# Running the later steps of eight attention items sooner, ahead of a woven MLP

## The chip, the cores and the metric

The kernel runs on one core of one Trainium2 chip. The metric is the device time of one execution in microseconds (us). PE is the matmul engine, DVE the vector engine, ACT the scalar engine, POOL GpSimd, SP the sync engine that issues most of the loads.

## What is computed

Causal attention with a decay bias, then a dense MLP with leaky ReLU, then a mixture of four experts that all see every token. Heads are joined into 1152 tokens of width 512 between attention and MLP.

```python
def _attn_ref(q, k, v, s):                      # q, k, v: (2, 8, 576, 64), s: (2, 8, 576)
    scores = scale * np.matmul(q, k.transpose(0, 1, 3, 2))
    cum = np.cumsum(np.maximum(s, 0.0), axis=-1)
    bias = -(cum[:, :, :, None] - cum[:, :, None, :])
    scores = np.where(causal, -1e9, scores + np.minimum(bias, 0.0))
    attn = np.exp(scores - np.max(scores, axis=-1, keepdims=True))
    attn = attn / (np.sum(attn, axis=-1, keepdims=True) + 1e-09)
    return np.matmul(attn, v)

def _moe_ref(x, w_in, w_out):                   # 512 -> 2048 -> 512
    h = x @ w_in
    return np.maximum(0.01 * h, h) @ w_out

def _moe2_ref(x, domain_probs, w1, w2):         # 4 experts, 512 -> 1024 -> 512
    p = domain_probs / (domain_probs.sum(-1, keepdims=True) + 1e-09)
    for e in range(4):
        out += p[:, e:e + 1] * (np.maximum(x @ w1[e], 0.0) @ w2[e])
```

## The kernel before

**Parts.** The tokens of each batch are cut into a first part (positions 0 to 255, two tiles of 128) and a second part (256 to 575, three tiles). A *unit* is one pair of heads of one batch in one part. Units 0 to 7 are the first part, units 8 to 15 the second. A unit is cut into *items*, one row tile of one head, or the short last tile of both heads together: four items in a unit of the first part (items 0 to 31), five in one of the second (items 32 to 71). Item 27 ends unit 6, item 31 ends unit 7 and with it the first part.

**Steps of an item** (class `Unit`). `scores` (line 691) multiplies on PE into a bank `ps_sc` (two of these) and lets DVE add the mask and take the row minimum of the negated scores. `exps` (line 718) is one ACT instruction. `transposes` (line 722) turns the tile on PE into a bank `ps_pt` (two of these, shared with `finish`), and ACT copies it out. `values` (line 732) multiplies with the values on PE into the one bank `ps_o`; at the last item of a unit DVE then divides by the row sums (`st`, `xo`). `finish` (line 749), which does something at the last item of a unit only, transposes the unit's output on PE (`ps_x`, a bank of `ps_pt`) and ACT writes it as the MLP's input `x`. `second_term` (line 770), for the first part and its last items only, lets DVE compute the rounding rest of that input, and counts the unit as done. None of these last four steps issues a DMA.

**Order.** All of this part is written into the engines in one order given by hand (`InOrder`, line 33): each engine works through its instructions strictly as they are written. `attention` (line 783) is a generator that counts i up from 0. At each i it writes `scores` of item i, `second_term` of item i - 8, `exps` of item i - 1, yields; `transposes` of item i - 3, yields; `values` of item i - 5, `finish` of item i - 7, yields. The list is `STEPS` (line 781); i runs to 79. Loads of keys and values follow i alone.

**First loop** (line 841). It draws the three yields of each i. Into the second one it puts one of nine early steps of the MLP (`OPENED`), which need only heads that are done; the tenth step needs the last pair of heads. From i = 31 it also puts one small matmul on zeros into the first and the second yield (`onto_held`, line 572: 128 columns, added onto a bank in use, where it changes nothing). After the third yield it advances the weight supply by one step from i = 31 on. It ends at the third yield of the i at which all eight units of the first part are done: `done == 2 * NP`.

**Weight supply.** `supply` (line 139) turns the 16 pieces of the first MLP's weights from 64-bit floats into 32-bit: ACT makes a first version, DVE works over it in four steps (`raw`), ACT's queue stores the piece to DRAM (`w_f`) and fetches the raw 64-bit bytes of a later piece. If the MLP is to use it soon, the piece is split at once into two terms (`w`). If not, `late_splits` (line 118) loads it back later by SP's queue and splits it. Piece 15 goes this second way.

**Second loop** (line 866). It draws the rest of attention, and per i weaves in about 2.12 steps of the MLP on the first part's tokens (`main`, 128 steps in all, three matmuls of 512 columns each), one to three supply steps and two of `late_splits`. It is called the weave below.

**Third loop** (line 885). It draws what is left of `main` with a count m from 0. At even m it advances `late_splits`; at every fourth m the ten steps of `tokens` (`paired_steps`, line 364), which prepare the second part's tokens for the next MLP on ACT and DVE (`sums` on DVE, `t` on both); at odd m from 5 the steps of `first_sevens` (line 213), which load two pieces by SP (pieces 16 and 17), add and subtract blocks of them on POOL (`sums`) and split them on ACT and POOL (`w`). What is left of either is written after the loop.

In `main`, the last parts are a down-projection (steps 88 to 103, results added to `y` by DVE), two hidden tiles (steps 104 to 111, evicted as `ht` by ACT and DVE), and the last down-projection (steps 112 to 127), which needs both hidden tiles and piece 15. Piece 15 may be split only once step 104 has been reached.

**Behind it** lies the MLP on the second part's tokens (matmuls `ps_u<-t,w`) and then the experts, ordered by a scheduler from its own estimates rather than by hand. The second of the seven products with which it begins needs the last step of `tokens`.

Of the kernel before, what the change touches and what calls it, by code (L numbers as in the profile page):

```python
# [19 lines left out]
def attention_moe_moe2(ctx: ExitStack, tc: tile.TileContext, q, k, v, s, w_in, w_out, probs, w1, w2, out):  # L20
# [36 lines left out]
    NP = H // 2  # L57
# [564 lines left out]
    def load_keys(n, queue=None):  # L622

        b, hp, i0, i1 = of_unit(n)
        q0, q1 = tiles[i0][0], tiles[i1 - 1][2]
        heads = slice(2 * hp, 2 * hp + 2)
        k_of = k[b, heads, :, :q1].rearrange("h d s -> d h s")
        q_of = q[b, heads, :, q0:q1].rearrange("h d s -> d h s")
        if i0 == 0:
            nc.sync.dma_start(k_e[n % 3][:D], k_of)  # L630
            (queue or nc.sync).dma_start(q_e[n % 3][:D], q_of)
        else:
            qr = ap.tile([P, 2, QC], F32, tag="qr", name="qr")
            for part in (slice(0, D), slice(D, P)):
                nc.sync.dma_start(qr[part, 0], q_of[:, 0])
                nc.sync.dma_start(qr[part, 1, LAST:], q_of[:, 1, : QC - LAST])
                nc.sync.dma_start(qr[part, 1, :LAST], q_of[:, 1, QC - LAST :])
            kr = ap.tile([P, 2, S], F32, tag="kr", name="kr")[:D]
            nc.sync.dma_start(kr, k_of)
            k_raw[n] = qr, kr  # L640

    def load_values(n, queue=None):
        b, hp, i0, i1 = of_unit(n)
        q1, rows, vs = tiles[i1 - 1][2], slice(hp * P, (hp + 1) * P), v_s[n % 4]
        full = min(q1 // P, QT - 1)
        (queue or nc.sync).dma_start(vs[:, :full, 1 : 2 * D + 1], v[b, : full * P, rows].rearrange("(t p) c -> p t c", p=P))
        if i1 == QT:
            nc.sync.dma_start(vs[P - S % P :, QT - 1, 1 : 2 * D + 1], v[b, full * P :, rows])
# [3 lines left out]
    def split_keys(n):  # L652

        b, hp = of_unit(n)[:2]
        qr, kr = k_raw.pop(n)
        qs = q_s[n % 2]
        ks, kd = (ap.tile([P, 2, S], F32R, tag=tag, name=tag) for tag in ("ks", "kd"))
        decay(n, kd)
        nc.gpsimd.dma_start(kd[:D], k[b, 2 * hp : 2 * hp + 2].rearrange("h d s -> d h s"))
        nc.scalar.copy(qs[:, 0, :, :QC], qr)  # L660
        yield
        nc.vector.tensor_tensor(qs[:D, 1, :, :QC], qr[:D], f32(qs[:D, 0, :, :QC]), ALU.subtract)
        for j in range(2):
            nc.scalar.copy(ks[:D, j], kr[:, j])
            yield
            nc.vector.tensor_tensor(ks[D:, j], kr[:, j], f32(ks[:D, j]), ALU.subtract)
        k_split[n] = ks, kd, qs
        yield

    def decay(n, kd):  # L670

        b, hp, i0, i1 = of_unit(n)
        q1, h = tiles[i1 - 1][2], b * H + 2 * hp
        if i0 == 0:
            nc.sync.dma_start(kd[D : D + 1], cum[h : h + 2, :q1])
        else:
            nc.sync.dma_start(f32(kd[D:DK, :, :q1]), cum_d[:, h : h + 2, :q1])
# [101 lines left out]


    STEPS = ((Unit.scores, 0), (Unit.second_term, 8), (Unit.exps, 1), (Unit.transposes, 3), (Unit.values, 5), (Unit.finish, 7))

    def attention():

        nonlocal ending
        items, starts, n = [], {}, 0
        i, split = 0, iter(())
        while n < units or i < len(items) + 8:
            if n < units and i == len(items):
                u = Unit(n)  # L790
                starts[n] = i
                items += [(u, *of) for of in u.items]
                if n + 2 < units and not 0 <= n + 2 - 2 * NP < 2:
                    load_keys(n + 2)
                    if n + 2 < 2 * NP:
                        decay(n + 2, k_e[(n + 2) % 3])
                if n in (2 * NP - 4, 2 * NP - 2):
                    load_keys(n + 4 if n == 2 * NP - 4 else n + 3)
                n += 1
            if n < units - 1 and i == starts[n - 1] + 2:  # L800
                load_values(n + 1)
            if i == starts[n - 1] and 2 * NP <= n < units:
                split = split_keys(n)
            for step, lag in STEPS:
                if 0 <= i - lag < len(items):
                    u, *of = items[i - lag]
                    step(u, *of)
                if lag == 1:
                    next(split, None)
                if lag in (1, 3, 7):  # L810

                    late = i - 5 + (lag == 7)
                    ending = lag != 3 and 0 <= late < len(items) and items[late][1:] == items[late][0].items[-1]
                    yield i
            i += 1
# [9 lines left out]
    with ExitStack() as phase:  # L825
# [5 lines left out]

        CONVERTING = (*range(5, 16), *range(17, 31, 2))
        side, units_of_w, late, opened = attention(), supply(), late_splits(), 0
        nothing = ps_mm.tile([P, 512], F32, tag="mm", name="nothing")
        with tc.tile_pool(name="early", bufs=1) as early:
# [5 lines left out]
            for at_ in range(3 * 64):  # L841
                i = next(side)
# [112 lines left out]
```

## Time and profile before

| what | us |
|---|---|
| median of three runs | 720.54 |
| the three runs | 717.39, 720.54, 970.85 |
| the profiled execution | 717.48 |
| its span in the profile | 715.70 |
| outside the span | 1.78 |
| end of the first loop (scores of item 40 begin on PE) | 69.55 |
| last matmul of attention begins | 195.96 |
| the next MLP begins on PE | 228.38 |

Times inside the profile count from the start of the span. A line of a timeline has start and duration, engine, operation with output and inputs, and how many instructions of a kind were merged (x3); square brackets hold the idle time of the engine before it and what ended that. All instructions bear the line of one helper (L43), so they are told apart by the names of their tiles. A matmul of plain 32-bit floats shows as two records, so an `onto_held` shows as x2.

### The profile page before, as it was taken

How to read it: one execution, taken by the hardware profiler on the slowest of the kernel's cores; microseconds unless marked ns; L12 is line 12 of the kernel's file. 1: busy time of each engine (PE TensorE's matmuls, PEld its weight loads, DVE VectorE, ACT ScalarE, POOL GpSimd, SP SyncE). 2: the span in 40 equal slices, each digit the busy share in tenths (PEclk: the TensorE clock that was granted, in tenths of full speed). 3: DMA queues.
4: the chain of work that ended last, by engine and by line, in shares of the span. 5: the costliest groups of instructions: out<-in, count | busy, mean ns of one | idle time of the engine just before them, and what ended most of it. 6: DMA issues, size and time to landing. Idle time of an engine off the chain costs nothing.

```text
span 715.7 us, 11167 instructions
## 1 busy us (share of the span) xinstructions
PE 696.9 (97%) x4256; PEld 633.2 (88%) x4256; DVE 433.7 (61%) x867; ACT 315.1 (44%) x640; POOL 253.9 (35%) x232
## 2 busy tenths in 40 slices
PE   8899999999988999999999999999999999999998
PEld 8778888888877999999988989889899898898986
DVE  7778788897767657735943634435435454364452
ACT  5757977875644574624422413323223142141210
POOL 6000000000039787964382522804526137142200
PEclk9999999999999999999999999999999999999999
DMA  9877688746442321320211211102011011010002
GB/s 232 207 195 208 194 211 245 220 143 235 177 177 61 118 82 66 119 60 30 60 60 31 59 31 59 60 1 89 31 57 54 8 60 60 1 59 1 1 36 97
DMA packets 43124, 69.61 MB, mean 97 GB/s; under 512 B 5616, under 2 KB 24832, under 8 KB 43072
## 3 DMA queue, kind: packets, MB, share of 16 engines
q1 hardware_dynamic: 32544, 40.83, 20.0%
q10 hardware_dynamic: 9376, 25.73, 10.6%
q0 software_dynamic: 1152, 2.36, 1.9%
q8 instruction: 33, 0.54, 0.3%
q14 instruction: 19, 0.16, 0.1%
HBM read 58.06 MB, written 10.82 MB: 96 GB/s over the span
## 4 chain that ended last, share of the span: by engine, by line
PE 82%; DVE 7%; DMA 4%; ACT 2%; POOL 2%; issue 1%; SPq 0%; ACTq 0%; POOLq 0%; DVEq 0%
PE ps_d L43 39%; PE ps_u L43 34%; PE ps_o L43 4%; PE ps_sc L43 3%; PE ps_pt L43 2%; DVE raw L43 2%; DMA qe<-in_q_dram 1%; DVE t L43 1%; ACT w L43 1%; DVE z L43 1%; DMA vs<-in_v_dram 1%; DMA raw<-w_f 1%; DMA ke<-in_k_dram 1%; DVE w L43 1%; POOL sums L43 1%
## 5 line engine op out<-in xcount | busy, mean ns | idle before, releaser
L43 PE MATMUL ps_u<-t,w 128*128 128x320 f32 (+1 forms) x1680 | 236.5, 299 | 1.1 <-DVE t L43 1.1
L43 PEld LDWEIGHTS ps_u<-t,w 128*128 128x128 f32 x1680 | 233.0, 189 | 4.8 <-DVE t L43 1.4
L43 PE MATMUL ps_d<-w,ht 128*128 128x512 f32 (+1 forms) x876 | 203.4, 388 | 0.0
L43 PEld LDWEIGHTS ps_d<-w,ht 128*128 128x128 f32 x876 | 161.0, 188 | 31.5
L43 POOL TENSOR_TENSOR w<-raw,w 128x512 fp32r<-128x512 f32 (+2 forms) x72 | 108.0, 1522 | 218.9 <-ACT w L43 218.9
L43 ACT ACTIVATE ht<-ps_u 128x320 fp32r<-128x320 f32 (+2 forms) x176 | 74.4, 433 | 153.7 <-DVE ps_u L43 129.0
L43 PE MATMUL ps_d<-ht,w 128*128 128x320 f32 (+1 forms) x576 | 111.0, 343 | 4.7 <-DVE ht L43 2.8
L43 DVE SCALAR_TENSOR_TENSOR oacc<-ps_d,pn,oacc 128x512 f32<-128x512 f32 (+1 forms) x64 | 47.5, 742 | 104.0 <-PE ps_d L43 104.0
L43 ACT CAST w<-raw 128x512 fp32r<-128x512 f32 (+2 forms) x94 | 64.5, 722 | 87.4 <-PE ps_d L43 67.7
L43 PEld LDWEIGHTS ps_d<-ht,w 128*128 128x128 f32 x576 | 92.3, 190 | 12.0 <-DVE ht L43 3.2
L43 DVE SCALAR_TENSOR_TENSOR ht<-ps_u,ht 128x320 fp32r<-128x320 f32 (+1 forms) x128 | 56.3, 452 | 23.3 <-ACT ht L43 22.0
L43 DVE TENSOR_TENSOR ps_u<-ps_u,tmp 128x320 f32<-128x320 f32 (+1 forms) x120 | 56.2, 471 | 23.3 <-PE ps_u L43 21.7
L43 POOL TENSOR_TENSOR sums<-raw 128x256 f32<-128x256 f32 x48 | 38.4, 818 | 66.1 <-PE ps_d L43 64.6
L43 DVE TENSOR_TENSOR tmp<-ps_u,tmp 128x320 f32<-128x320 f32 (+1 forms) x80 | 36.8, 463 | 40.4 <-PE ps_u L43 39.4
L43 POOL TENSOR_TENSOR w<-sums,w 128x1024 fp32r<-128x1024 f32 x24 | 58.2, 2424 | 5.3 <-ACT w L43 5.3
L43 PEld LDWEIGHTS ps_o<-vs,pv 128*128 128x128 f32 x400 | 53.5, 191 | 6.8 <-issue 2.3
L43 PE MATMUL ps_u<-x,w 128*128 128x512 f32 x192 | 56.3, 410 | 0.9 <-DVE x L43 0.9
L43 PE MATMUL ps_o<-vs,pv 128*128 128x65 f32 (+1 forms) x400 | 53.3, 267 | 2.1 <-DVE xo L43 1.2
L43 POOL DMA_DIRECT2D kd<-in_k_dram x8 | 4.8, 603 | 127.3 <-PE ps_sc L43 67.0
L43 ACT ACTIVATE z<-z,mn 128x256 f32<-128x256 f32 (+4 forms) x72 | 42.4, 588 | 12.0 <-DVE mn L43 7.2
L43 DVE CUSTOM_DVE_ANT_0 z<-ps_sc,mask 128x256 f32<-128x256 f32 (+4 forms) x72 | 36.0, 501 | 12.5 <-PE ps_sc L43 9.7
L43 ACT COPY pv<-ps_pt 128x512 f32<-128x512 f32 (+3 forms) x80 | 33.2, 424 | 21.2 <-PE ps_pt L43 20.7
(78 smaller groups left out, 647.0 us busy)
## 6 DMA issues: line engine op xcount, KB each, us to landing
raw<-in_moe_w_dram SPq DMA_DIRECT2D x32, 512.0 KB
raw<-w_f SPq DMA_DIRECT2D x22, 512.0 KB
r<-in_moe_w_in_dram ACTq DMA_DIRECT2D x8, 1024.0 KB
w_f<-raw ACTq DMA_DIRECT2D x16, 512.0 KB
r<-in_moe_w_out_dram ACTq DMA_DIRECT2D x8, 1024.0 KB
kd<-in_k_dram POOLq DMA_DIRECT2D x8, 288.0 KB, 6.0
kr<-in_k_dram SPq DMA_DIRECT2D x8, 288.0 KB
vs<-in_v_dram SPq DMA_DIRECT2D x8, 256.0 KB
```

What stands on the lines that cost most here:

```text
L43: ins = call(*args, **kw)
```

## The change

A function `sooner` says for items 24 to 31 (`left` from 7 down to 0) by how many i a step is drawn forward. For items 24 to 28: `values`, `finish` and `second_term` by one. For items 29 to 31: `transposes` by one, `values` by two, `finish` and `second_term` by three. `scores` and `exps` stay, and every other item stays. `attention` keeps for each step the next item that is due, and runs as many as are due.

```diff
     STEPS = ((Unit.scores, 0), (Unit.second_term, 8), (Unit.exps, 1), (Unit.transposes, 3), (Unit.values, 5), (Unit.finish, 7))
+    FIRST = 4 * 2 * NP
+
+    def sooner(n, step):
+
+        left = FIRST - 1 - n
+        if not 0 <= left < 8 or step in (Unit.scores, Unit.exps):
+            return 0
+        if left < 3:
+            return 1 if step is Unit.transposes else 2 if step is Unit.values else 3
+        return int(step is not Unit.transposes)
 
     def attention():
...
+        due = [0] * len(STEPS)
         while n < units or i < len(items) + 8:
...
-            for step, lag in STEPS:
-                if 0 <= i - lag < len(items):
-                    u, *of = items[i - lag]
+            for s, (step, lag) in enumerate(STEPS):
+                while due[s] < len(items) and i - due[s] >= lag - sooner(due[s], step):
+                    u, *of = items[due[s]]
                     step(u, *of)
+                    due[s] += 1
```

Unit 7 is therefore done at i = 36 and no longer at i = 39, and the first loop ends there.

## Rows read from the trace of the kernel before

**Rows 1.** Page: busy time, share of the span and instructions of each engine.

```profile
PE 696.9 (97%) x4256; PEld 633.2 (88%) x4256; DVE 433.7 (61%) x867; ACT 315.1 (44%) x640; POOL 253.9 (35%) x232
```

**Rows 2.** Windows by stage: length, busy PE, PEld, DVE, ACT, POOL; PE clock, DMA share, GB/s.

```profile
61.83:69.55 7.72, 7.72 (x65) 7.48 (x64) 6.96 (x17) 5.82 (x12) 0.02 (x1) 1.00 0.64 152
69.55:196.20 126.65, 124.59 (x783) 108.86 (x783) 105.76 (x197) 93.36 (x171) 2.90 (x5) 1.00 0.67 203
196.20:228.40 32.20, 27.53 (x115) 21.86 (x114) 23.99 (x32) 13.21 (x23) 20.16 (x17) 0.95 0.39 132
```

**Rows 3.** Timeline of PE, items 35 and 36.

```profile
57.60 0.66 PE L43 MATMUL ps_pt<-ident,z 128*128 128x128 f32 x4 [0.40 <-ACT pv L43]
59.18 0.30 PE L43 MATMUL ps_pt<-ident,z 128*128 128x128 f32 x1 [0.92 <-DVE x L43]
...
60.01 0.38 PE L43 MATMUL ps_u<-idle 128*128 128x128 f32 x2
60.23 0.33 PE L43 MATMUL ps_o<-vs,pv 128*128 128x65 f32 x2
```

**Rows 4.** Groups of DVE by form, 69.55 to 196.2 us: busy us, mean ns, idle before.

```profile
L43 DVE TENSOR_TENSOR ht<-ps_u,ht 128x512 fp32r<-128x512 f32 x14 | 9.6, 688 | 7.7 <-ACT ps_u L43 7.5
...
L43 DVE TENSOR_TENSOR w<-raw,w 128x1024 fp32r<-128x1024 f32 x7 | 8.6, 1224 | 4.5 <-ACT w L43 4.5
...
L43 DVE TENSOR_SCALAR raw<-raw 128x1024 f32<-128x1024 f32 x12 | 8.2, 686 | 0.0
```

**Rows 5.** Timeline of PE, end of the weave to the next MLP.

```profile
193.09 0.95 PE L43 MATMUL ps_u<-x,w 128*128 128x512 f32 x3
...
196.21 3.68 PE L43 MATMUL ps_d<-ht,w 128*128 128x512 f32 x15
201.76 5.71 PE L43 MATMUL ps_d<-ht,w 128*128 128x512 f32 x24 [1.88 <-DVE y L43]
207.31 5.60 PE L43 MATMUL ps_u<-x,w 128*128 128x512 f32 x24
212.75 2.71 PE L43 MATMUL ps_d<-ht,w 128*128 128x512 f32 x11
218.25 10.29 PE L43 MATMUL ps_d<-ht,w 128*128 128x512 f32 x37 [2.79 <-DVE ht L43]
```

**Rows 6.** Chain that ended last, 198 to 218 us: start, duration, what.

```profile
198.32 2.63 DMA w_f<-raw
...
201.45 5.91 DMA raw<-w_f
...
207.92 0.75 POOL sums L43
...
211.98 1.05 ACT w L43
...
214.23 3.37 DVE t L43
```

**Rows 7.** Timeline of ACT, 204 to 232 us.

```profile
207.38 1.66 ACT L43 CAST w<-raw 128x512 fp32r<-128x512 f32 x3 [7.24 <-DMA raw<-w_f]
...
221.16 1.05 ACT L43 CAST w<-sums 128x1024 fp32r<-128x1024 f32 x1 [5.14 <-POOL sums L43]
...
223.10 1.26 ACT L43 CAST t<-sums 128x1280 fp32r<-128x1280 f32 x1
```

**Rows 8.** Timeline of all engines, start of the next MLP.

```profile
228.38 11.89 PE L43 MATMUL ps_u<-t,w 128*128 128x320 f32 x80
...
229.19 1.69 DVE L43 TENSOR_TENSOR t<-sums,t 128x1280 fp32r<-128x1280 f32 x1
```

**Rows 9.** Windows of 4 us behind the second wait, columns as in rows 2.

```profile
216.00:220.00 4.00, 1.75 (x4) 1.41 (x5) 3.96 (x5) 0.01 (x1) 3.84 (x4) 0.80 0.28 57
220.00:224.00 4.00, 4.00 (x15) 3.19 (x14) 2.45 (x6) 2.84 (x4) 4.00 (x5) 0.78 0.02 3
```

**Rows 10.** Timeline of PE, 332 to 358 us, where the experts begin.

```profile
349.35 5.33 PE L43 MATMUL ps_u<-t,w 128*128 128x320 f32 x33 [1.15 <-DVE t L43]
```

## The prediction

> **What bounds the kernel now.** I read the page's busy shares first, then the windows by stage, then the timelines of PE and DVE where the first loop ends, and last the chain and the timelines where attention hands over to the next MLP. PE is busy 97% of the span [rows 1], so time is won only by taking work from PE or by closing a hole in it. The stages differ. In items 37 to 39, the last three of the first loop, PE has no hole in 7.72 us, yet six of its matmuls are fillers on zeros; DVE is busy for 6.96 of it [rows 2]. In the weave PE is busy 124.59 of 126.65 us. From its end to the next MLP, PE is busy 27.53 of 32.20 us, at a mean granted clock of 0.95 [rows 2]. There lie the two largest holes, 1.88 us for a bank that DVE frees and 2.79 us for a hidden tile that DVE finishes late [rows 5]. Behind the second, 37 matmuls take 10.13 us, 0.274 each, where 24 took 5.55, 0.231 each [rows 5]: the granted clock was 0.80 and 0.78 in the two stretches of 4 us there [rows 9], a mixture of its levels of 1.2 and 2.4 GHz.
>
> The chain says what set this. Piece 15's store leaves ACT's queue at 198.32 and takes 2.63; SP's load behind it takes 5.91; POOL's sums begin at 207.92; ACT splits them at 211.98, then casts `t`; DVE's `t` takes 3.37, and the hidden tile stands behind it [rows 6]. ACT itself stood 7.24 us for that load [rows 7].
>
> **The change part by part.**
>
> *The moved steps.* The same transposes, values and finishes run, none with a DMA, and they pass nothing but scores and fillers on PE. Item 31's `second_term` falls from i = 39 to 36, so the first loop ends three items sooner. Six fillers (two per i) go. From one pair's start to the next instruction is 60.23 - 60.01 = 0.22 us [rows 3]: 6 x 0.22 = 1.3 us off PE.
>
> *Items 28 to 36.* Two holes at item 35 should close: 0.40 us for a copy of ACT and 0.92 us for the bank that item 27's `second_term` frees [rows 3], now one item sooner. Gain at most 1.3. Against it, the division of unit 7 and item 31's rest now come to DVE before item 37 begins.
>
> *Items 37 to 39.* Seven steps of `main` join them: the weave runs 43 items instead of 40, at 2.12 steps. A step is 5.55 / 8 = 0.69 us [rows 5], so 4.8 us of PE work come here from the third loop. On DVE the stage gains three hidden tiles (3 x 0.69), one split (1.22) and two passes over a raw piece (2 x 0.69) [rows 4], 4.7 us, and loses unit 7's division and item 31's rest, together between nothing and as much as one split: 6.96 + 4.7 less 0 to 1.2 is 10.5 to 11.7 us beside 7.72 - 1.3 + 4.8 = 11.2 us of PE. DVE is all but full: its debt, with what items 28 to 36 leave it, costs PE between nothing and 1.2 us, one split. I take 0.6, the middle. With 0.6 of the possible 1.3 gained before, the front end nets 0, between -1.3 and +1.2.
>
> *DMA and weights.* Supply steps run sooner: three fewer in the first loop, seven more in the weave, so the supply is four steps ahead at a given i. Their stores and fetches on ACT's queue and the loads back on SP's move along, past attention's key loads. The DMA engines are 0.64 and 0.67 busy there [rows 2]: I cost this at nothing. Piece 4 is split two items ahead of its use where it was three; without that cover PE would wait for one split.
>
> *The third loop.* At the weave's end PE had 35 steps left from 197.6 us (196.21, and two steps of item 79 still of the weave). Without waits the next MLP would begin at 197.6 + 35 x 0.69 = 221.8; it began at 228.4 [rows 8]: 6.6 us lost in holes and clock. Now the weave ends at 197.6 - 1.3 + 4.8 = 201.1 with 28 steps left: 220.4 without waits. That is the ceiling, 8.0 us.
>
> What holds it back is the chain. Piece 15's store stood at item 78's second yield; four supply steps sooner, it stands at item 76's third. PE was there at 193.1 [rows 5], now 3.5 later, 196.6, 1.7 before 198.32. Loads land at 205.7 (207.4 less 1.7), POOL's first sums end at 210.3. The hidden tiles leave PE at m = 7 and m = 11, about 206.6 and 209.4, and now stand on ACT and DVE ahead of POOL's split and of the long `t`, since the counts m kept their places and `main` moved seven steps: both large holes should go. ACT splits piece 16 no sooner than before, having the second tile ahead of it; POOL, through its first sums 1.7 sooner, ends the second ones between 0 and 1.7 before 221.16 [rows 7]. I take 0.7, nearer to ACT's end: 220.4. From there ACT ends the last cast of `t` 3.2 later, as before (223.10 + 1.26 - 221.16 [rows 7]), at 223.6, and DVE the last `t` at 223.6 + 1.7 = 225.3 [rows 8]. Before, that came at 230.9, 2.5 us after the next MLP had begun, and delayed nothing. Now it is late next: PE arrives at 220.4, has 2.5 us of other products, and waits until 225.3, for 2.4 us. It gains 228.4 - 222.8 = 5.6 us. That new wait may bring the lower clock, which cost 37 x 0.043 = 1.6 after a like wait [rows 5, 9]; nothing at best. I take 0.6. Three steps of `tokens` are now left over after the loop instead of one: their time is in this sum.
>
> **Sum.** 5.6 - 0.6 + 0 = 5.0 us off the profiled execution's 717.5 (span 715.7 and 1.8 around it): 712.5 us. The median of the runs shown is 720.54, 3.1 above that execution, and one of the three stands far off, so I sum from the execution. Two per cent, 14 us, is what a measurement can tell here; nothing in this sum reaches it.
>
> The Trainium skill ("SBUF — State Buffer", Who interferes with whom) says that a DVE instruction with two SBUF inputs and a GpSimd instruction that reads SBUF take turns, whoever issued first holding the port to its end. The two long `t` of this trace, 3.37 and 1.69 us [rows 6, 8], are in keeping with that; it speaks against ending on a `t` beside POOL, and gives the second rival below.
>
> **Rivals.**
>
> *Only the fillers.* The third loop loses what it lost before, in other places: DVE's debt of 1.2 us carries through the weave, and the store is held there. For it: DVE is the engine nearest to full at the front. Against it: DVE is busy 105.76 of 126.65 us in the weave [rows 2], so a debt is paid back. Time: 717.5 - 1.3 = 716.2, up to 1.0 either way.
>
> *The last `t` meets POOL.* The long `t` of DVE took 3.37 us at 214.23, where POOL was at work nearly throughout, and 1.69 at 229.19 [rows 6, 8, 9]. After the change the last one falls at 223.6, when POOL still splits piece 17. If it takes 3.4 again, the next MLP waits 1.7 longer: 714.2. Against it: POOL may be through by then.
>
> *The handover hides everything.* The last `t` and the sums come soon enough, or the scheduler puts other products ahead: the whole 8.0 and the front's 1.3: 708.2. For it: the first products behind the loop ran 2.5 us before the last `t` already. Against it: after the load POOL's sums alone take 4.1 us (207.92 to 211.98), and there are two pieces, the second of which ACT awaited for 5.14 us [rows 6, 7].
>
> *Slower: the load at the handover lands late.* PE gets there with seven steps less to cover the chain from store to `t`. The place is the start of the next MLP. If loads land at 207.4 + d, the last `t` ends at 225.3 + 1.7 + d = 227.0 + d and the next MLP, 2.5 ahead of it, effectively begins at 224.5 + d: from d = 3.9 this is later than before. The weave's end moves by 3.5, so a store that kept its place behind it gives d = 3.5; one us of DVE or DMA delay more decides. With d = 5.5, the wait of over 9 us and a lower clock behind it at twice the price (3.2), the time is 717.5 + 1.6 + 3.2 = 722.3. For it: that load and store are on the chain now [rows 6]. Against it: the store is four supply steps ahead in the order, whatever the clock does.
>
> *It does not do what it says:* transposes of items 29 to 31 must find `exps` of the item before done; ACT had holes there, so I give it no chance of its own.
>
> **How the numbers follow.** Forecast 0.42, its own range 710 to 714; only the fillers 0.20; the `t` beside POOL 0.13; everything hidden 0.10; slower 0.15. The range 708.0 to 720.5 holds the front's bounds, the clock's price, the first three rivals and a part of the slower case, and leaves some 0.15 out. Faster by over 2% (under 706.1) would need more than the ceiling and the front together: 0.02. Slower by over 2% (over 735) needs a weight that comes far too late or another order behind the third loop: 0.04. Within: 0.94.
>
> **What would show it.** Fillers 24 records instead of 36; item 40's scores at about 73 instead of 69.55; no hole at item 35; piece 15's store near 196.6; the holes of 1.88 and 2.79 gone, a new one of 2 to 3 us for DVE's `t` at the start of the next MLP, which begins near 220; from then on everything 5 us sooner. I am wrong if the store is not sooner, if PE waits for DVE in items 37 to 39 by more than 1.2 us, or if the part ordered by the scheduler comes out in another order: no row prices that, the nearest is its hole of 1.15 us [rows 10], so I bound it by 1.2 either way and take nothing.

## The result and the profile after

The changed kernel took 730.39 us, the median of four runs (725.35 to 732.35), beside 719.64 us before: a ratio of 1.0146, 95% interval 1.0114 to 1.0177. It is slower, clear of the noise but by less than 2%, and not the 712.5 us forecast. A ratio compares whole sets of runs, is not the quotient of two medians, and leaves out two runs in a slower state, 970.85 us before and 728.40 us in r7 below. Its profiled execution took 730.22 us with a span of 728.4.

Stages by PE's timeline, from one mark to the next, with what the prediction's steps make of each (us):

| stage | before | after | difference | predicted |
|---|---|---|---|---|
| start to item 37 | 61.8 | 64.6 | +2.8 | -0.6 |
| item 37 to attention's last output transpose | 134.1 | 144.4 | +10.3 | +4.1 |
| from there to the next MLP's first product | 32.4 | 22.6 | -9.8 | -11.5 |
| from there to its first down-projection | 12.3 | 19.5 | +7.2 | +3.0 |
| from there to the experts | 93.3 | 95.6 | +2.3 | 0 |
| experts to the end | 381.7 | 381.7 | 0 | 0 |
| sum | | | +12.8 | -5.0 |

The page's busy line (as rows 1): 12 matmul records are gone, as the six fillers should take, and PE's share fell to 96%.

```profile
PE 699.6 (96%) x4244; PEld 635.1 (87%) x4244; DVE 440.5 (60%) x867; ACT 315.0 (43%) x640; POOL 253.5 (35%) x232
```

Windows of the kernel after, with the columns of rows 2: items 37 to 39, the weave, the third loop, then a piece of the weave, and two pieces of the start of the next MLP.

```profile
64.60:75.12 10.52, 10.52 (x70) 9.15 (x68) 8.94 (x19) 9.23 (x16) 0.55 (x1) 1.00 0.74 140
75.12:209.30 134.18, 127.82 (x784) 111.43 (x783) 108.13 (x199) 90.87 (x166) 2.89 (x5) 0.97 0.64 195
209.30:231.62 22.32, 21.44 (x97) 17.46 (x95) 15.70 (x21) 8.77 (x17) 12.61 (x11) 1.00 0.42 141
100.00:105.00 5.00, 4.17 (x17) 3.80 (x18) 3.15 (x8) 3.64 (x8) 0.00 (x0) 0.66 1.00 369
...
236.00:240.00 4.00, 0.62 (x2) 0.40 (x3) 4.00 (x4) 3.21 (x6) 3.90 (x3) 0.72 0.16 64
240.00:244.00 4.00, 4.00 (x16) 4.00 (x17) 2.60 (x2) 0.75 (x2) 4.00 (x3) 0.50 0.39 135
```

Items 37 to 39 are dense: PE has no hole. The weave is not: PE idles 6.4 of 134.18 us, where it idled 2.1 of 126.65 [rows 2], and its clock is granted at 0.97 in the mean, where it was 1.00: from 100 to 105 us, behind a hole of 2.31 us, it is 0.66. The third loop is nearly closed, as meant: 0.88 us idle instead of 4.67.

PE's timeline of the kernel after, with its largest holes (as rows 3, 5 and 8):

```profile
47.66 0.63 PE L43 MATMUL ps_o<-vs,pv 128*128 128x65 f32 x4 [1.12 <-DVE xo L43]
...
63.17 0.44 PE L43 MATMUL ps_x<-ident,xo 128*128 128x128 f32 x2 [1.28 <-ACT pv L43]
...
100.83 0.77 PE L43 MATMUL ps_pt<-ident,z 128*128 128x128 f32 x4 [2.31 <-ACT pv L43]
...
158.47 0.33 PE L43 MATMUL ps_sc<-ks,qs 128*128 128x128 f32 x1 [1.71 <-DVE mn L43]
...
212.48 2.97 PE L43 MATMUL ps_d<-ht,w 128*128 128x512 f32 x12 [0.88 <-DVE y L43]
215.29 5.60 PE L43 MATMUL ps_u<-x,w 128*128 128x512 f32 x24
220.73 11.05 PE L43 MATMUL ps_d<-ht,w 128*128 128x512 f32 x48
231.62 3.24 PE L43 MATMUL ps_u<-t,w 128*128 128x320 f32 x21
237.30 0.41 PE L43 MATMUL ps_u<-t,w 128*128 128x320 f32 x1 [2.44 <-DVE y L43]
239.79 11.51 PE L43 MATMUL ps_u<-t,w 128*128 128x320 f32 x62 [2.08 <-DVE t L43]
```

Of the holes of rows 5, the first shrank from 1.88 to 0.88 us and the second is gone: 48 matmuls run through at 220.73. The holes of rows 3 at item 35 are gone too, but two others opened (47.66 and 63.17). In the weave lie five above 0.3 us, two of them shown, together 6.3 us; before, there were four, together 1.7. And 21 products into the next MLP PE stands twice, 4.5 us in all, after which its clock is granted at 0.72, then 0.50, the lower level of 1.2 GHz.

What DVE did at that place (its timeline; POOL's follows):

```profile
225.36 3.22 DVE L43 TENSOR_TENSOR t<-sums,t 128x1280 fp32r<-128x1280 f32 x1 [0.49 <-ACT t L43]
...
231.86 1.56 DVE L43 TENSOR_TENSOR sums<-x 128x320 f32<-128x320 f32 x1
233.34 1.02 DVE L43 TENSOR_TENSOR sums<-x,sums 128x320 f32<-128x320 f32 x1
234.29 2.35 DVE L43 TENSOR_TENSOR pn<-pn,prow 128x36 f32<-128x36 f32 x1
236.56 0.68 DVE L43 TENSOR_TENSOR y<-ps_d,y 128x512 f32<-128x512 f32 x1
237.16 3.50 DVE L43 TENSOR_TENSOR t<-x,t 128x640 fp32r<-128x640 f32 x2
240.59 2.02 DVE L43 TENSOR_TENSOR t<-sums,t 128x1280 fp32r<-128x1280 f32 x1
```

```profile
231.78 2.24 POOL L43 TENSOR_TENSOR w<-raw,w 128x512 fp32r<-128x512 f32 x2
233.98 2.61 POOL L43 TENSOR_TENSOR w<-sums,w 128x1024 fp32r<-128x1024 f32 x1
236.69 2.36 POOL L43 TENSOR_TENSOR w<-raw,w 128x1024 fp32r<-128x1024 f32 x1
```

DVE runs without a gap from 225.36 to 242.6. The `y` that frees PE's bank and the `t` that PE needs stand in its queue behind the last `sums`, behind a product of 36 elements that takes 2.35 us, and behind each other. So "DVE y" and "DVE t" are the names at PE's holes, and the reading is that the whole queue is the cause; the experiments on the handover test it. With its window ended at 239.6 us, the timeline shows the first of the two `t<-x` by itself:

```profile
237.16 2.57 DVE L43 TENSOR_TENSOR t<-x,t 128x640 fp32r<-128x640 f32 x1
```

It ends at 239.73, and PE's second hole at 239.79. The last `t` (240.59 to 242.61) ends no hole of PE.

Last, one hole of the weave from near: timeline of all engines around the 2.31 us at 100.83.

```profile
97.11 1.22 DVE L43 SCALAR_TENSOR_TENSOR raw<-r,raw 128x1024 uint32<-128x1024 uint32 x1
...
98.36 0.34 ACTq L43 DMA_DIRECT2D w_f<-raw  x1
...
98.75 0.46 ACTq L43 DMA_DIRECT2D r<-in_moe_w_out_dram  x1
...
99.24 1.04 ACT L43 CAST w<-raw 128x1024 fp32r<-128x1024 f32 x1 [2.21 <-DVE mn L43]
...
100.20 0.74 ACT L43 COPY pv<-ps_pt 128x512 f32<-128x512 f32 x2
```

DVE's last pass over a raw piece ends at 98.33. ACT's store of that piece leaves at 98.36, so ACT had stood for it; the fetch and the split of 1.04 us come next, and only then the copy `pv` for which PE waits. The name in brackets, `mn`, is not what ACT waited for. Two more of the five holes are built like this, those of 1.05 us at 147.97 and of 1.71 us at 158.47. The stores ahead of them:

```profile
144.38 0.35 ACTq L43 DMA_DIRECT2D w_f<-raw  x1
...
154.76 0.34 ACTq L43 DMA_DIRECT2D w_f<-raw  x1
```

Each leaves 0.03 us behind the end of DVE's last pass, and ACT had been idle for 1.33, 0.54 and 1.15 us directly ahead of the three stores. Behind the third, DVE too waits 0.73 us, for ACT's split, and PE waits for DVE.

### The profile page after: what moved, and what is told of

It reads as the page before. It is cut to its first block, busy times and chain, and to the rows that moved or that the text cites. A ratio compares the mean times of both kernels' runs of the same rounds, so it can differ in the third digit from the quotient of the medians.

```text
span 728.4 us, 11139 instructions
## 1 busy us (share of the span) xinstructions
PE 699.6 (96%) x4244; PEld 635.1 (87%) x4244; DVE 440.5 (60%) x867; ACT 315.0 (43%) x640; POOL 253.5 (35%) x232
## 3 DMA queue, kind: packets, MB, share of 16 engines
q1 hardware_dynamic: 32544, 40.83, 19.6%
q10 hardware_dynamic: 9376, 25.73, 10.3%
## 4 chain that ended last, share of the span: by engine, by line
PE 70%; DVE 9%; ACT 3%; issue 2%; POOL 2%; DMA 0%; ACTq 0%; DVEq 0%; POOLq 0%
PE ps_d L43 36%; PE ps_u L43 29%; PE ps_o L43 3%; DVE t L43 2%; ACT w L43 2%; PE ps_sc L43 1%; DVE raw L43 1%; DVE sums L43 1%; POOL w L43 1%; PE ps_pt L43 1%; DVE ht L43 1%; DVE y L43 1%; DVE w L43 1%; DVE z L43 1%; ACT ht L43 1%
## 5 line engine op out<-in xcount | busy, mean ns | idle before, releaser
L43 PE MATMUL ps_u<-t,w 128*128 128x320 f32 (+1 forms) x1680 | 239.8, 301 | 7.3 <-DVE t L43 3.2
L43 DVE TENSOR_TENSOR tmp<-ps_u,tmp 128x320 f32<-128x320 f32 (+1 forms) x80 | 36.8, 463 | 40.6 <-PE ps_u L43 35.4
L43 POOL TENSOR_TENSOR sums<-raw 128x256 f32<-128x256 f32 x48 | 38.8, 827 | 61.8 <-ACT w L43 60.5
L43 POOL DMA_DIRECT2D kd<-in_k_dram x8 | 5.1, 636 | 138.3 <-PE ps_sc L43 138.1
```

Source lines behind the costliest of these rows:

```text
L43: ins = call(*args, **kw)
```

## The experiments

All ratios are to the kernel before, run beside each, with 95% intervals. The marks are those of the table above (us; "weave" is from item 37 to attention's last output transpose):

| kernel | time | ratio | weave | third loop | to first down-projection | to experts |
|---|---|---|---|---|---|---|
| before | 719.6 | | 134.1 | 32.4 | 12.3 | 93.3 |
| changed | 730.4 | 1.0146 [1.0114, 1.0177] | 144.4 | 22.6 | 19.5 | 95.6 |
| r0, changed again | 725.8 | 1.0107 [1.0063, 1.0152] | 139.2 | 22.6 | 19.6 | 95.7 |
| r1, loop to 39 | 719.4 | 1.0002 [0.9983, 1.0021] | 134.0 | 32.2 | 12.3 | 93.3 |
| r14, loop to 38 | 719.3 | 1.0003 [0.9987, 1.0018] | 135.0 | 25.7 | 13.8 | 99.1 |
| r15, loop to 37 | 719.8 | 1.0001 [0.9981, 1.0022] | 136.2 | 23.9 | 17.7 | 94.1 |
| r2, supply held back | 730.0 | 1.0141 [1.0113, 1.0169] | 141.5 | 23.6 | 20.4 | 95.7 |
| r4, slower weave | 723.8 | 1.0063 [1.0025, 1.0102] | 141.0 | 28.4 | 12.3 | 94.5 |
| r3, tokens paced | 719.8 | 1.0004 [0.9976, 1.0031] | 141.8 | 22.7 | 14.0 | 93.3 |
| r5, probabilities later | 725.9 | 1.0098 [1.0071, 1.0125] | 141.5 | 22.6 | 15.9 | 95.8 |
| r7, r3 and r5 | 720.1 | 1.0041 [1.0007, 1.0075] | 141.2 | 22.6 | 13.3 | 93.8 |
| r6, before, paced | 721.9 | 1.0054 [1.0031, 1.0077] | 134.4 | 35.4 | 12.3 | 93.3 |
| r12, before, 91 steps | 723.2 | 1.0068 [1.0040, 1.0097] | 140.3 | 21.9 | 19.0 | 95.7 |
| r8, paced, extra step at 1 | 721.3 | 1.0019 [0.9991, 1.0047] | 144.2 | 22.6 | 14.0 | 93.4 |
| r9, paced, extra step at 2 | 722.1 | 1.0055 [1.0028, 1.0083] | 141.8 | 22.6 | 14.0 | 93.4 |
| r10, changed, extra step at 1 | 729.3 | 1.0125 [1.0081, 1.0169] | 141.0 | 22.6 | 19.6 | 95.6 |
| r11, before, extra step at 1 | 718.1 | 0.9980 [0.9951, 1.0009] | 134.7 | 32.1 | 12.3 | 93.3 |
| r16, before, store later | 717.0 | 0.9983 [0.9961, 1.0006] | 132.6 | 31.0 | 12.3 | 94.7 |
| r17, changed, store later | 720.7 | 1.0026 [1.0007, 1.0046] | 135.6 | 22.6 | 18.9 | 95.7 |
| r13, paced, store later | 712.9 | 0.9910 [0.9878, 0.9941] | 134.1 | 22.6 | 14.0 | 93.5 |

The time is the median of the runs, the stages are those of the one profiled execution. The front, from the start to item 37, is not in the table: it took 61.3 to 66.7 us, and 67.7 in r17, whose profiled execution (724.1 us) was its slowest.

Moved work and fillers alone would make the changed weave 134.1 + 4.8 - 1.3 = 137.6 us. I call that due.

### The same program again

> The changed kernel itself, once more, for a second trace. Its first trace was already 2.0 us behind the trace of before at item 28, where nothing differs in the program yet, so that part should be chance: here the lead or lag at item 28 should lie anywhere between -2 and +2 us. What belongs to the change should come back: 7 us of holes and lower clock in the weave, 5 us or more lost at the start of the next MLP, time 725 to 732.

725.8 us. The eight runs of this program fall into two groups, four at 725.4 to 725.9 us and four at 730.2 to 732.4; each of the two profiles is of one group. The weave was 5.2 us shorter than in the first profile, the stages behind it the same to 0.1. Of the 5.2 us, 1.8 are holes (4.5 instead of 6.4); the rest is PE's busy time, 134.7 instead of 138.1 us, at a mean granted clock of 1.00 instead of 0.98. Where the first profile had a hole of 2.31 us and a clock of 0.66 behind it, this one has a hole of 1.30 (99.47) and keeps its clock:

```profile
100.00:105.00 5.00, 5.00 (x35) 4.53 (x34) 4.58 (x13) 3.29 (x7) 0.00 (x0) 1.00 1.10 296
```

So the loss in the weave differs between executions (1.6 to 6.8 us over what is due), more by the clock than by the holes; the loss at the handover does not.

### The moved steps alone, and how far the loop may shorten

```diff
-                if done == 2 * NP and at_ % 3 == 2:
+                if done == 2 * NP and i == 39 and at_ % 3 == 2:    # r1
+                if done == 2 * NP and i >= 38 and at_ % 3 == 2:    # r14; r15 with 37
```

> The steps of items 24 to 31 are moved as in the change, but the first loop still ends at i = 39, so that weave, supply and third loop stand where they stood before. If the moved steps themselves cost (a wait of 1.1 us for the one bank ps_o at item 28), and nothing else, the time is that of before or up to 2 us more: 718 to 722. If the moved steps are the cause of the whole loss: 727 or more. If only the shifted weave loses: as before, 717 to 721.

719.4 us: the moved steps alone are not told apart from no change, within 0.2% or 1.5 us either way. The traces see a small loss: from item 28 to item 37 it is 19.8 us in each of the 15 profiles with moved steps, and 18.6 to 19.5 in the five without. The large loss comes from the three items by which the loops shift.

> The changed kernel whose first loop ends at i = 38: one item of overlap given to the weave instead of three, third loop 33 steps. Theory that each item of shift costs by itself (the supply's lead and the main steps out of their places): the weave is 1.5 us longer by its added steps and about 2 us by holes, the first down-projection of the next MLP comes 12 to 14 us behind its first product, time 717 to 720 us. Rival (any shift meets bad places at once, the amount does not grow with it): weave 4 to 7 us over what is due already, time 721 to 725 us.

> The changed kernel whose first loop ends at i = 37: two items given to the weave, third loop 31 steps. Theory that each item of shift costs by itself: holes in the weave about 4 us over what is due, the first down-projection 13 to 17 us behind the first product of the next MLP, time 719 to 724 us, between the run with 38 and the changed kernel. Rival (any shift meets bad places at once): 724 to 728 us, the weave's share as large as in the changed kernel.

719.3 and 719.8 us, the times of the first theory, but not by its working. The weave takes what is due for one and for two items of shift (two and four more steps, two and four fewer fillers: 135.0 and 136.0 us): nothing is lost there by the first two, and 1.6 to 6.8 us by the third. At the start of the next MLP the loss does grow with the shift: 12.3, 13.8, 17.7, 19.5. With 38 most of the third loop's gain is there, and 5.8 us are lost again inside the next MLP: in one hole of 2.92 us, which a hidden tile from ACT ends (240.29), and in the 93 matmuls behind it, which took 0.178 us each where such took 0.148 before, 2.7 us, at a granted clock of 0.82.

### The weave: first attempts

```diff
-            if (at_ % 3 != 1 or i % 3 == 0) and not ending:
+            if (at_ % 3 != 1 or i % 3 == 0) and not ending and (i > 39 or at_ % 3 == 2):    # r2
-                owed += WOVEN * KD / (2.0 * (40 - 6))
+                owed += 84.5 / 86.0    # r4
```

> As the change, but in items 37 to 39 the supply takes one step per item, so that from item 40 on each of its steps falls on the same item as before the change; the MLP stays seven steps ahead. Theory A (the weave loses because the supply's ACT instructions, which wait for DVE's passes, now stand in front of other copies of attention): the holes of 6.3 us in the weave go, 723 to 725. Theory B (the weave loses because the MLP's steps run ahead): holes stay, 728 to 732. Theory C (the loss is at the handover): stays, or more, since piece 15's store comes later: 730 to 735.

> As the change, but the weave draws 84 steps of the MLP over its 43 items (0.98 per yield instead of 1.06), as many as it drew over 40 before the change, so that the third loop has its 35 steps again; the supply stays four steps ahead. If the handover loses because PE comes to it with seven steps less to cover the tokens (cover theory), the loss there goes and the fillers' 1.3 us are won: 716 to 721, with holes in the weave of 0 to 4 us deciding where in it. If the supply's lead is what costs: 725 or more. If the density of the weave makes its holes, they go too: 716 to 718.

r2: 730.0 us. With the supply put back to its old place the holes moved, to 95.14 and 138.57 among others, and PE now waited for weights as well; their sum was 4.7 us, beside 6.4 and 4.5 in the two profiles of the changed kernel. r4: with main's steps spread as before over the longer weave, 84 instead of 91, the weave was 141.0 us where 134.1 - 1.3 = 132.8 were due. Its two largest holes, 2.39 us at 96.75 and 2.40 at 143.14, again lie behind a store that leaves 0.03 us behind DVE's last pass (94.30, 138.76). So neither the supply's lead alone nor the density of main's steps alone makes the holes. But r4, with 35 steps left for the third loop, has the 12.3 us back at the handover.

```diff
-            if (at_ % 3 != 1 or i % 3 == 0) and not ending:
+            if (at_ % 3 != 1 or i % 3 == 1) and not ending:    # r8, r10, r11; r9 with 2
```

> The change with the tokens paced, and with the weave's extra supply step (the one after the second yield) at i mod 3 = 1 instead of 0. Written out, a piece's store and split on ACT stand 3 yields (one whole item) behind its last pass on DVE for every piece split at once before the change, but only 2 behind for pieces 4, 6, 9, 10 and 12 after it, because the whole supply moved against the extra steps. With mod 1 every distance is 3 or more again. Gap theory (ACT waits for DVE's last pass, and PE for the copies behind it on ACT): the weave's holes at pieces 9 and 10 (1.0 and 1.7 us) go, and 3 us of the 4 that the weave takes over its due: 715 to 718. If the position of the split against the items, not the gap, makes the holes: 718 to 723.

> The same with the extra step at i mod 3 = 2: now pieces 3, 4, 5, 6, 8 and 10 have a distance of 2 yields. Gap theory: at least as many holes as with mod 0, in other places, 719 to 724, and slower than mod 1 by 3 us or more. Otherwise no order between the three.

> The change with only the extra supply step moved to i mod 3 = 1; tokens as in the change. If weave and handover are two separate losses that add up: the weave gains 3 us or more, the handover still loses its 7, so 722 to 725, about 5 to 8 over the paced kernel with the same supply. If the handover follows from the weave's lateness: as fast as that one.

> The kernel before with the extra supply step at i mod 3 = 1. There it is mod 1 that gives distances of 2 yields (pieces 4, 5, 6, 9) where mod 0 has 3. Gap theory: the weave of the kernel before gets the holes that the change got, 3 us or more slower than before, 721 to 726. If mod 1 is simply better or worse placed for all kernels: it moves this one the same way as the changed one.

721.3, 722.1, 729.3 and 718.1 us: moving the supply's every-third-item step by one or two items neither mends the changed weave (141.0 to 144.2) nor harms the one before. r8 gives every piece its three yields again and keeps holes of 5.2 us; r11 takes a yield from four pieces and has 2.3 us, as the kernel before has 2.1. The theory that two or three yields between DVE's last pass and ACT's store decide it falls.

### The weave: a whole step between DVE's last pass and ACT's store

In the weave, a piece's store and direct split are written behind the next piece's first DVE pass instead of ahead of it (`heading` is true in the first loop only).

```diff
             yield
-            if last:
+            if last and heading:
                 yield from finished(*last)
                 yield
+                last = None
-            last = n, raw
             nc.vector.tensor_scalar(raw, raw, 2.0, LARGEST, ALU.max, ALU.min)
             yield
+            if last:
+                yield from finished(*last)
+                yield
+            last = n, raw
```

> The changed kernel with tokens paced over the third loop; in the weave the store and the direct split of a piece are written one supply step later (behind the next piece's first DVE pass instead of ahead of it), so that ACT meets them with DVE's last pass longer done. Theory that ACT's queue, held by a store or a split that waits for DVE, makes the holes of the weave: from item 37 to the last transposed output 137.6 to 139 us instead of 141.8, time 715 to 717 us. Rival (the holes come with which items and evictions fall together, and a step later only moves them): 141 to 143 us, time 719 to 721 us.

> The kernel before with the store and the direct split one supply step later in the weave; nothing else. If ACT's queue behind DVE's last pass is what made holes, the kernel before, which had 1.7 us of them in the weave, gains 1 to 2 us there: from item 37 to the last transposed output 132 to 133 us instead of 134.1; piece 15's store, one step later, keeps the third loop at 32 us; time 715 to 718 us. Rival (the later store is worth as much without the moved steps, and the faster run before owes them nothing): 712 to 714 us.

> The changed kernel with the store and the direct split one supply step later in the weave, and tokens at every fourth m as in it (no pacing). Theory that the two losses are separate: the weave 134 to 136 us as in the run with both edits, third loop 22.6, the first down-projection of the next MLP 19.5 us behind its first product and 95.6 from there to the experts, as in the changed kernel: 712.9 + 5.5 + 2.2 = about 720 us. Rival (the later store alone mends both): 713 to 715 us.

The weave fell to 134.1 us (r13) and 135.6 (r17), under what is due, since the kernel before had holes of its own there (r16: 132.6). Two groups of the weave, ACT's direct splits and PE's transposes, with their idle time behind the second bar, show why. The kernel after:

```profile
L43 ACT CAST w<-raw 128x1024 fp32r<-128x1024 f32 x7 | 7.3, 1049 | 7.4 <-DVE mn L43 5.2 <-DVE raw L43 1.4 <-ACT pv L43 0.4
...
L43 PE MATMUL ps_pt<-ident,z 128*128 128x128 f32 x144 | 23.0, 278 | 4.2 <-ACT pv L43 4.2
```

The same of r13, then of r16:

```profile
L43 ACT CAST w<-raw 128x1024 fp32r<-128x1024 f32 x9 | 9.5, 1051 | 2.3 <-DVE mn L43 1.6 <-issue 0.4 <-ACT pv L43 0.3
...
L43 PE MATMUL ps_pt<-ident,z 128*128 128x128 f32 x143 | 21.8, 272 | 0.0
```

```profile
L43 ACT CAST w<-raw 128x1024 fp32r<-128x1024 f32 x7 | 7.4, 1052 | 0.8 <-DVE qs L43 0.5 <-issue 0.3
...
L43 PE MATMUL ps_pt<-ident,z 128*128 128x128 f32 x143 | 21.9, 273 | 0.1
```

ACT's idle time ahead of the direct splits falls from 7.4 to 2.3 us, and PE's for `pv` from 4.2 to 0.0. In the kernel before it is 3.0 and 1.3, in r16 0.8 and 0.1. All holes of the weave together fall from 6.4 us to 0.1 (r13) and 1.1 (r17), and in both ACT is at work until each store of the weave leaves. That ACT's queue, held behind DVE's last pass, makes most of these holes is shown. The edit moves the store and the direct split together, so which of the two matters more is not. In r13 and r17 two more pieces are split directly than in the changed kernel (nine instead of seven in the weave), but that is not it: r2 and r12 had eleven, and were 3.9 and 1.4 us over their due.

r13 is 3.5 us under due. The 2.1 us of holes that the kernel before had explain a part. The other 1.4 us are not explained; due may be that much too high, since it reckons each step at 0.69 us.

r10 seems to speak against this: ACT's idle time ahead of its splits was 3.0 us, as low as in the kernel before, and it still had 5.2 us of holes. The largest, 2.85 us at 154.12, again lies behind a store that leaves 0.03 us behind DVE's last pass (151.65), by one long wait instead of several. At the other two (1.64 us at 83.73, 0.68 at 137.14) PE waits for `mn` while DVE is at its passes over raw pieces, at the first for two in a row (2.47 us from 80.73). So there is a second cause beside ACT's queue. What is open: why three items of shift make the passes fall badly and one or two do not.

### The handover

```diff
-            if m % 4 == 0:
+            if m % 5 in (0, 2):    # r3, and r6 on the kernel before
                 next(tokens, None)
```

> As the change, but the third loop advances the tokens at two of five m instead of one of four, so that all ten steps lie inside its 28 m instead of three behind it. Theory C (the next MLP starts late because the last tokens and what DVE has in front of them come late): the holes of 2.4 and 2.1 us and part of the lower clock at the start of the next MLP go, 723 to 727. Theories A and B, by which the weave sets the loss: the start of the next MLP improves by no more than 1 us, 728 to 731. If the earlier tokens delay the hidden tiles on DVE instead: up to 733.

> The kernel before with the tokens paced as in the run before that paced them (two of five m). Control: there one token step was left over behind 35 m, and the next MLP had no hole at its start. If the pacing only repairs what the change broke: no gain, 717 to 721. If it is a gain by itself, which the change hides: 714 to 717. Earlier tokens in front of the hidden tiles may cost: up to 723.

r3: 719.8 us; 14.0 instead of 19.5 us to the first down-projection, and the 2.3 us inside the next MLP are gone as well. All ten token steps now lie within the 28 steps of main. PE's timeline there:

```profile
229.47 4.86 PE L43 MATMUL ps_u<-t,w 128*128 128x320 f32 x32
235.70 7.89 PE L43 MATMUL ps_u<-t,w 128*128 128x320 f32 x52 [1.38 <-DVE y L43]
```

One hole instead of two, and 52 products at 0.152 us each, where 62 took 0.186 in the kernel after. On the kernel before the same edit costs 3 us in the third loop (r6: 35.4), where the token steps then stand ahead of the hidden tiles: PE waits 2.65 us for `y` and 3.80 for `ht`, instead of 1.88 and 2.79 [rows 5]. So the pacing is no gain in itself.

`probabilities()`, which gives `prow` and `pn` on DVE, moved behind the next MLP's steps:

```diff
     fixed = False
-    probabilities()
...
+    probabilities()
     paired_tokens(1, y_t[1], t7pool)
```

> As the change, but the expert probabilities (loads, and four small DVE instructions) are written behind the MLP on the second part instead of before it. In the second trace of the change these four take 3.5 us of DVE among the last additions to y and the last t, up to 2.35 us for 36 elements, while POOL works. If DVE's queue at the handover is what the next MLP waits for, and these stand in it: 2 to 3.5 us less than the changed kernel, 722 to 726. If POOL's or ACT's chain sets the handover: the same as the changed kernel, 726 to 730.

> The change with the tokens paced and the probabilities written later. With the pacing alone the next MLP still waited 1.4 us at its start for an addition to y behind the probabilities' instructions, and reached its first down-projection 14.0 us after its begin, where it took 12.3 before. If these stand in the way: 1 to 2 us less than the paced kernel's 719.8, so 717 to 719. If not: 719 to 721.

r5: 725.9 us, with 15.9 us: taking the slow `pn` out of DVE's queue gives 3.7 of the 7.2 us, and nothing of the 2.3 inside. r7: 720.1 us, 13.3, only 0.7 us less than r3 alone: both relieve the same queue, and the hole of 0.67 us that is left ends with a `w` of POOL. In both runs the later place costs something elsewhere: from the experts to the end they took 383.7 us, 2.0 more than before (all other profiles: 381.6 to 382.0), which is more than r7 gains over r3 at the handover.

Last, whether the moved steps have any part in it. The kernel before, whose weave draws as many steps as the changed one's:

```diff
-                owed += WOVEN * KD / (2.0 * (40 - 6))
+                owed += 91.5 / 80.0
```

> The kernel before, whose weave draws 91 steps of main over its 40 items where it drew 84; no step of an item is moved. The third loop then has 28 steps, as in the changed kernel. Cover theory (the handover loses because 28 steps cover fewer of the ten steps of tokens and of the POOL work): from the next MLP's first product to its first down-projection 18 to 20 us instead of 12.3, from there to the experts about 95.6 instead of 93.3; weave from item 37 to its last transposed output 134.1 + 4.8 = 138.9 us or a little over; next MLP 22.6 us behind that. Sum: 717.4 + 4.8 - 9.8 + 7.2 + 2.3 = 722 us and more by what the weave adds. Rival (the handover's loss belongs to the moved steps or to the supply's lead): the 12.3 and 93.3 stay, and the time is 712 to 716 us.

723.2 us. With no step moved, 28 steps in the third loop give the same two holes and the same 19.0 us, against the rival's 12.3, and 95.7 inside. PE's timeline of r12:

```profile
224.59 3.24 PE L43 MATMUL ps_u<-t,w 128*128 128x320 f32 x21
230.42 0.41 PE L43 MATMUL ps_u<-t,w 128*128 128x320 f32 x1 [2.58 <-DVE y L43]
232.90 10.89 PE L43 MATMUL ps_u<-t,w 128*128 128x320 f32 x62 [2.07 <-DVE t L43]
```

21, 1 and 62 products as in the kernel after. That the handover loses because seven steps of cover are gone is shown from both sides, by r4 and by r12.

### What beats both

r13, the change with paced tokens and the later store, took 712.9 us, 0.9% faster than before, which is clear of the noise but less than 2%. Its two additions act separately: the later store alone mends the weave (r17: 135.6, and 18.9 at the handover), the pacing alone the handover (r3: 14.0, and 141.8 in the weave). The later store by itself on the kernel before is not told apart from no change (r16: 0.9983 [0.9961, 1.0006]). Both additions without the moved steps were not tried, so how much of the 0.9% needs those is open.

## Why the prediction was wrong

*The third loop, right but for 1.7 us.* Where the holes come from (piece 15's chain and the long `t` ahead of the hidden tile) and that seven steps of main fewer in front would close both was right: 32.4 fell to 22.6 us, against 20.9 forecast. What is left are the 0.88 us of the first hole and one step of main (0.7) more behind the last output transpose than I reckoned.

*The front, right as a balance only.* The fillers, the dense items 37 to 39 (10.5 us, where I had 11.2 and up to 1.2 more for DVE) and the closed holes at item 35 came as said. I did not see two new holes. Items 23 and 24 now bring their values one behind the other into the one bank `ps_o`, which waits 1.12 us for the division (47.66), and a transposed output waits 1.28 us for ACT (63.17). Item 37 began 2.8 us late, of which 2.0 were there at item 28 (44.79 instead of 42.76), up to which both kernels run the same program: item 28 began anywhere between 42.6 and 47.9 us in the 20 profiles, for a reason that stays open. The other 0.8 us belong to the moved steps, where I had a gain of 0.6.

*"Now the weave ends at 197.6 - 1.3 + 4.8 = 201.1": wrong.* This step took the pace of the weave as given. I looked for DVE's debt in items 37 to 39 and for a late weight, and cost the supply's lead at nothing because the DMA engines had room. The resource that gave way was ACT's strictly ordered queue: a store that stands for DVE's last pass holds back the copy `pv`, and with it PE. Measured: 1.6 to 6.8 us more than the sum, in holes and, in the slower of the two profiles, in a lower clock behind them. The kernel before showed it already, 3.0 us of ACT's idle time ahead of direct splits and 1.3 of PE's ahead of transposes, but I had read the weave's DVE groups, not ACT's.

*The store, late with the weave.* I expected piece 15's store at 196.6. ACT's timeline of the kernel after:

```profile
205.01 0.62 ACT L43 CAST w<-raw 128x512 fp32r<-128x512 f32 x1 [3.08 <-DMA raw<-w_f]
205.40 0.35 ACTq L43 DMA_DIRECT2D w_f<-raw  x1
...
231.85 1.05 ACT L43 CAST w<-sums 128x1024 fp32r<-128x1024 f32 x1 [5.70 <-POOL sums L43]
232.81 1.08 ACT L43 CAST t<-x 128x640 fp32r<-128x640 f32 x2
234.40 1.26 ACT L43 CAST t<-sums 128x1280 fp32r<-128x1280 f32 x1 [0.52 <-DVE sums L43]
```

It left at 205.40, 8.8 us later, in a weave that ended at 209.04 instead of 199.5, 9.5 later: against the weave the store was where the order put it, and PE had its last up- and down-projection without a wait for it.

*The wait at the start of the next MLP, right in its place and its engine, wrong in its cause and size.* I said that PE would wait there for the last `t` of DVE, 2.4 us and 0.6 for the clock. Measured: 4.5 us of holes (2.44 + 2.08), and 62 products at 0.186 us where before 80 took 0.149 [rows 8]: 62 x 0.037 = 2.3 us of clock. Up to ACT the chain came nearly as said. PE arrived at 231.62 and ACT split the second piece's sums at 231.85, where I had both at 220.4. ACT ended the last cast of `t` at 235.66, 3.8 us later instead of 3.2, since that cast waited for DVE's `sums` of the tokens. The step that failed is the next one, "DVE the last `t` at 223.6 + 1.7": it has DVE free when ACT ends. DVE ended that `t` at 242.61, 6.95 us behind ACT instead of 1.7, because `pn`, a `y` and two other `t` stood in its queue first. The kernel before had shown it: there DVE ended that `t` at 230.88, 6.5 us behind ACT's cast, which ended at 224.36 [rows 7, 8]. PE did not even wait for the last `t`: it waited for the `y` (its bank), and for a `t` whose cast ACT had ended by 233.89 and which DVE began at 237.16. Three token steps left over after the loop were named in the prediction, but not laid end to end on DVE.

*The rivals.* "Only the fillers" had the third loop lose what it lost before, and it did not; "the handover hides everything" had no wait there, and there were two. The slower case had the right place but another cause (a load that lands late); at the handover PE waited for no load. The second, DVE's `t` beside POOL, was right in kind and is part of the 7.2 us, but it was not the last `t` (2.02 us, 1.69 before) that POOL stretched most: `pn` took 2.35 us, and the `t` of 640 columns 2.57, where it took 0.81 before (225.64).

That the scheduler's part behind would cost nothing, 1.2 us at most, was also wrong: 2.3 us. Of these, 1.7 are two holes in that MLP, 0.36 us for a split of POOL (278.77) and 1.30 for a `tmp` of DVE (306.14). The same two are in r0, r2, r5, r10, r12 and r17, and in none of the runs with paced tokens. Why a late start brings them later on is open.

That r13 comes out at 712.9, near the forecast, is no support for it: r13 has two edits more.

## What to carry to other kernels

Work that is written into an ordered weave sooner does not only move; it takes cover away from what stays, so lay the queue of every engine at the handover end to end for the new number of covering steps. In such a weave, put at least one full step of other work between one engine's last pass and the instruction of another that waits for it, above all a store issued from the queue that also feeds PE. And when a shift loses time, look at the ordered queues of the engines that are far from busy first: ACT was 43% busy and held PE up.

## What the runs showed of the hardware

A small DVE instruction beside POOL took as long as POOL's still needed. The product `pn` of 36 elements took 2.35 us at 234.29, while POOL's split of 1024 columns ran from 233.98 to 236.59; it ended at 236.64. In the kernel before, the same product took 0.48 us, and there too it ended 0.04 us behind an instruction of POOL, of which only 0.44 us were left:

```profile
225.78 1.27 POOL L43 TENSOR_TENSOR sums<-raw 128x256 f32<-128x256 f32 x1
...
226.61 0.48 DVE L43 TENSOR_TENSOR pn<-pn,prow 128x36 f32<-128x36 f32 x1
```

The Trainium skill ("SBUF — State Buffer", Who interferes with whom) says that a DVE instruction with two SBUF inputs and a GpSimd instruction that reads SBUF take turns at a shared port. The rows agree: the price here is what is left of POOL's instruction, not the length of DVE's. I had applied that only to the long `t` of 1280 columns, which took 3.22 us at 225.36 beside POOL, and 1.49 in r3 at 218.70 with POOL idle.

The same program, executed twice, had 144.4 and 139.2 us in its weave, and four of the five holes came back (0.43, 1.30, 1.06 and 1.72 us). An order by hand with little slack between two engines turned small differences into 1.8 us more of holes. A lower granted clock behind two of them (0.66 from 100 to 105 us, 0.73 from 160 to 165), which the other execution did not have, came with another 3.4 us of PE's time.
